# Token rows by transposes, gate products in four column strips: the attention stage of a retention and mixture-of-experts kernel on Trainium2

## The chip, the cores and the metric

One Trainium2 chip, one core. The metric is the device time of one execution in microseconds (us), as a median of runs.

## What is computed

Three layers behind each other, all inputs and outputs in float32:

```python
scores = scale * (q @ k.T)                     # 8 batches, 8 heads, 576 tokens, 64 per head
ret    = scores * Dmat                         # Dmat[i, j] = gamma_h ** (i - j) for i >= j, else 0
x      = (ret @ v), heads side by side         # 4608 token rows of 512
logits = x @ w_gate                            # 8 experts
e      = argmax(logits); g = softmax(logits)[e]
x      = g * (relu(x @ w1[e]) @ w2[e])         # one expert per token
h      = x @ w_in; out = (h * cos(h)) @ w_out
```

## The kernel before

Four stages follow each other on TensorE: attention, the experts, the conversion of the last layer's weights beside them, and the last layer. The change lies in the attention stage, the first 175 us or so.

Attention runs over 40 steps (`steps`), one for each batch and each chunk of 128 tokens (the fifth chunk of a batch has 64). The order of the work is written out by hand: every engine works off its instructions in the order in which the loop at L724 issues them. In step i the loop calls

- `scores(i)` (L452): the products of keys and queries, sixteen float32 matmuls on 64x64 quarters of the array into two PSUM banks, which VectorE multiplies by the mask into `pT` (L466);
- `decay(i + 1)` (L443): the values of the next chunk times a factor per token and head, eight ScalarE multiplications (L449) into `vs`;
- `inter(i - 1)` (L477) and `intra(i - 1)` (L490): the state of earlier chunks times the queries (64x64 quarters, L487), then values times `pT` (two column halves of 64, L497); VectorE multiplies the sum by `gx` into `xt`, features by tokens (L500); L506 adds to the state, which ScalarE copies out (L509);
- `rows(i - 2)` (L511): `xt` is turned into token rows and multiplied by the gate's weights at once. Each of four float32 matmuls has `xt` as the weights and `wgi`, an identity of 128 columns with the 8 gate columns beside it, as the moving operand (L518). ScalarE copies the rows out (L520), VectorE adds up the logits (L521), and SyncE's queue sends the rows to `xd` in HBM (L523).

A float32 matmul stands in the trace as two pairs of weight load and matmul, so the four of L518 are eight records. Every five steps come `route`, `place`, `spread` and `table`, which rank the tokens by expert on VectorE, GpSimd and a few matmuls (L555 to L563, L637). All of `scores`, `rows` and the two blocks turned by `x_block` (L248) near the end take their PSUM banks in turn from one ring of four, tag "sc". Loads of q, k, v have five buffers; the load of step i + 4 is issued at the end of step i (L769), on SyncE's queue behind the rows of step i - 2. Before the loop, L700 to L720 issue the first loads, some memsets and 13 matmuls on zeros (`warm`).

Of the kernel before, what the change touches and what calls it, by code (L numbers as in the profile page):

```python
# [11 lines left out]
F32 = mybir.dt.float32  # L12
# [5 lines left out]
ALU = mybir.AluOpType  # L18
# [4 lines left out]
P = 128  # L23
H = 8
D = 64
DM = 512
E = 8
# [13 lines left out]
NWARM = 13  # L41

# [15 lines left out]
C_TRI = C_GF + NCH * 4  # L58
# [3 lines left out]
C_EYE = C_BASE + E  # L62
C_LO = C_EYE + E
# [40 lines left out]
def of_chunks(q, k, v):  # L104

    B, H_, S, D_ = q.shape

    def turned(x, o, n):
        t = x[:, :, o:o + n].reshape(B, H_ // 2, 2, n, D_).transpose(0, 2, 4, 1, 3)
        return t.reshape(B, 2 * D_, H_ // 2 * n)  # L110

    def rows(x, o, n):
        return x[:, :, o:o + n].transpose(0, 2, 1, 3).reshape(B, n, H_ * D_)

    full = np.stack([np.concatenate([turned(k, o, n), turned(q, o, n), rows(v, o, n), rows(k, o, n)], axis=2)
                     for o, n in CH[:-1]], axis=1)
    o, n = CH[-1]
    return full, np.concatenate([turned(k, o, n), turned(q, o, n)], axis=2), rows(v, o, n)


@with_exitstack
def attn_moe_kernel(ctx, tc, full, part, tail, wg, w1, w2, win, wout, ctab, out):
# [235 lines left out]
    with ExitStack() as actx:  # L358
# [7 lines left out]
        def cc(col, n, rows=P):  # L366
            return ca[:rows, col - C_MASK:col - C_MASK + n]
# [7 lines left out]
        wgs = ap1.tile([P, 4, E], F32, name="wgs")  # L375

        RW = P + E
        wgi = ap1.tile([P, 4, RW], F32, name="wgi")
# [10 lines left out]

        def setup_rows():  # L390
            nc.vector.tensor_copy(out=wgi[:, 0::2, 0:P], in_=ident.unsqueeze(1).to_broadcast([P, 2, P]))
            for a in range(2):
                nc.vector.tensor_copy(out=wgi[:, 1::2, a * D:(a + 1) * D],
                                      in_=ident[:, (1 - a) * D:(2 - a) * D].unsqueeze(1).to_broadcast([P, 2, D]))
            nc.vector.tensor_copy(out=wgi[:, :, P:RW], in_=wgs)
# [15 lines left out]
        for i in range(2):  # L411
            t = ap1.tile([P, NCH, 2, E], F32, name=f"lgt{i}")
            nc.gpsimd.memset(t, 0.0)
            lgt.append(t)
# [96 lines left out]
        def rows(i):  # L511
            b, c = steps[i]
            o, n = CH[c]
            x = ap3.tile([P, 4, P], F32, tag="xs", name="xs")
            for g in range(2):
                two = ps1.tile([P, 4, P], F32, tag="sc", name="rw", bufs=4).rearrange("p (j a) t -> p j (a t)", a=2)
                for j in range(2):
                    mm(out=two[:, j, 0:RW], lhsT=xts[i % 3][:, 2 * g + j, :], rhs=wgi[:, 2 * g + j, :], start=(j == 0),  # L518
                       stop=True, skip_group_check=True)
                nc.scalar.copy(out=x[:n, 2 * g:2 * g + 2], in_=two[:n, :, 0:P])  # L520
                nc.vector.tensor_reduce(out=lgt[b % 2][:n, c, g, :], in_=two[:n, :, P:RW].rearrange("p j e -> p e j"),  # L521
                                        axis=AX.X, op=ALU.add)
            nc.sync.dma_start(out=xd[b * SEQ + o:b * SEQ + o + n, :], in_=x[:n].rearrange("p j t -> p (j t)"))  # L523

# [3 lines left out]
        def route(i0, n):  # L528
# [3 lines left out]
            L = ap2.tile(sh, F32, tag="L", name="L")  # L532
            nc.vector.tensor_add(out=L, in0=lgt[b % 2][:, c0:c0 + n, 0, :], in1=lgt[b % 2][:, c0:c0 + n, 1, :])
# [177 lines left out]
        wgc = wg.rearrange("(c p) e -> p c e", p=P)  # L711
        nc.gpsimd.dma_start(out=wgs[:, 0::2], in_=wgc[:, 0::2])
        for a in range(2):
            nc.gpsimd.dma_start(out=wgs[a * D:(a + 1) * D, 1::2], in_=wgc[(1 - a) * D:(2 - a) * D, 1::2])
# [4 lines left out]
        warm(NWARM, ps1.tile([P, 8, P], F32, tag="x", name="xps").rearrange("p a t -> p (a t)"), idle)  # L719
        decay(0)  # L720
# [3 lines left out]
        for i in range(NS):  # L724
# [23 lines left out]
            if i >= 2:  # L748
                rows(i - 2)
# [684 lines left out]
```

## Time and profile before

| | |
|---|---|
| median of 3 runs | 1383.82 us (1382.86 to 1387.58) |
| the profiled execution | 1377.58 us, span 1375.3 us |
| TensorE matmuls busy | 1354.1 us, 98% of the span |
| TensorE weight loads busy | 1262.5 us, 92% |
| VectorE, ScalarE, GpSimd busy | 68%, 55%, 14% |
| granted TensorE clock, mean | 0.996 |
| moved by DMA | 300.58 MB, mean 219 GB/s |

The profile shows one execution, and its rows carry times from the span's start. PE is TensorE's matmuls, PEld its weight loads, DVE VectorE, ACT ScalarE, POOL GpSimd and SP SyncE. A matmul's duration in a row is its latency: matmuls overlap, so what one costs is read from start to start. A row for a stretch has its start and end, its length, the busy time of PE, PEld, DVE, ACT and POOL, each with its count of instructions, the granted TensorE clock, the busy share of the DMA engines and GB/s. A number in square brackets is idle time before, with what ended it.

### The profile page before, as it was taken

To read this page: it belongs to the slowest core of one execution; us is meant where nothing else is said; L and a number is where in the kernel's file an instruction comes from. 1 tells how busy PE (TensorE), PEld (TensorE's weight loads), DVE (VectorE), ACT (ScalarE), POOL (GpSimd) and SP (SyncE) were. 2 spreads that over 40 slices of the span, in tenths; PEclk is the share of its full clock that TensorE was granted. 3 is DMA by queue.
4 is the path that set the end of the run, shared out by engine and by line. 5 is a ranking of instruction groups with operands and counts; after the bars stand their busy time and mean duration, and the time that the engine had idled before them with its cause. 6 is when DMAs were issued, how large, how long until landed. Compare 5 with 4: busy or idle time off the path is not lost.

```text
span 1375.3 us, 28314 instructions
## 1 busy us (share of the span) xinstructions
PE 1354.1 (98%) x11234; PEld 1262.5 (92%) x11234; DVE 939.5 (68%) x1928; ACT 757.2 (55%) x1687; POOL 191.0 (14%) x300
## 2 busy tenths in 40 slices
PE   7999999999999999999999999999999999999998
PEld 6888899999999999998999999999999999999997
DVE  4777865867778687847666676766767676666655
ACT  5788725444544455336556555555555555555544
POOL 4334530121211212100010100101001010010101
PEclk9999999999999999999999999999999999999999
DMA  8899626575876668976564655646455564564551
GB/s 290 320 329 346 213 61 217 180 262 183 285 246 203 211 230 268 331 275 259 176 258 164 220 190 191 220 166 249 183 192 201 194 233 161 209 226 162 196 184 57
DMA packets 72648, 300.58 MB, mean 219 GB/s; under 512 B 7748, under 2 KB 15904, under 8 KB 58560
## 3 DMA queue, kind: packets, MB, share of 16 engines
q1 hardware_dynamic: 60000, 256.18, 53.0%
q0 software_dynamic: 12512, 42.56, 8.3%
q8 instruction: 89, 1.46, 0.4%
q14 instruction: 47, 0.39, 0.1%
HBM read 247.24 MB, written 51.47 MB: 217 GB/s over the span
## 4 chain that ended last, share of the span: by engine, by line
PE 49%; issue 6%; POOL 0%; POOLq 0%; ACT 0%
PE acc L1341 25%; PE hps L1265 24%; POOL out_dram L1323 0%; POOLq L1430 0%; ACT ka L1295 0%; POOL spare L159 0%; PE acc L1352 0%; POOLq L1323 0%; ACT orow L1321 0%
## 5 line engine op out<-in xcount | busy, mean ns | idle before, releaser
L1341 PE MATMUL acc<-wunit,gh 128*128 128x512 f32 x1152 | 358.2, 392 | 0.0
L1265 PEld LDWEIGHTS hps<-far,wquad 128*128 128x128 f32 x2064 | 261.8, 191 | 8.0 <-ACTq L1239 0.7
L1265 PE MATMUL hps<-far,wquad 128*128 128x256 f32 x2064 | 266.7, 283 | 0.5 <-ACTq L1239 0.5
L1341 PEld LDWEIGHTS acc<-wunit,gh 128*128 128x128 f32 x1152 | 207.2, 189 | 36.0
L1341 PE MATMUL acc<-wunit,gl 128*128 128x512 f32 x576 | 224.3, 389 | 0.0
L274 PE MATMUL hps<-xT,wunit 128*128 128x256 f32 (+6 forms) x1536 | 209.4, 297 | 0.5 <-ACT yev L291 0.5
L274 PEld LDWEIGHTS hps<-xT,wunit 128*128 128x128 f32 x1536 | 206.7, 188 | 0.9 <-ACT yev L291 0.7
L289 PE MATMUL hps<-hh,wunit 128*128 128x256 f32 (+6 forms) x960 | 197.9, 301 | 0.0
L289 PEld LDWEIGHTS hps<-hh,wunit 128*128 128x128 f32 x960 | 155.8, 190 | 0.1
L289 PE MATMUL hps<-hl,wunit 128*128 128x256 f32 (+6 forms) x480 | 143.5, 299 | 1.4 <-DVE hl L278 1.4
L1323 POOL DMA_INDIRECT out_dram<-orow,perm x36 | 35.4, 982 | 740.3 <-DVE orow L1319 736.4
L1341 PEld LDWEIGHTS acc<-wunit,gl 128*128 128x128 f32 x576 | 108.2, 188 | 24.5 <-DVE gl L1308 0.8
L1306 ACT CAST gh<-sa 128x512 fp32r<-128x512 f32 x144 | 89.6, 622 | 72.9 <-DVE sa L1302 72.9
L1302 DVE SCALAR_TENSOR_TENSOR sa<-sa,box 128x512 f32<-128x512 f32 x144 | 99.0, 688 | 42.8 <-ACT sa L1300 41.7
L1265 PE MATMUL hps<-near,wquad 128*128 128x256 f32 x960 | 126.6, 283 | 0.0
L1265 PEld LDWEIGHTS hps<-near,wquad 128*128 128x128 f32 x960 | 123.1, 191 | 3.6
L1276 DVE TENSOR_TENSOR box<-hps,box 128x256 f32<-128x256 f32 x72 | 30.6, 424 | 136.7 <-PE hps L1265 136.5
L1308 DVE TENSOR_TENSOR gl<-sa,gh 128x512 fp32r<-128x512 f32 x144 | 98.9, 687 | 18.5 <-ACT gh L1306 12.9
L1297 DVE SCALAR_TENSOR_TENSOR sa<-box,ka 128x512 f32<-128x512 f32 x144 | 98.9, 687 | 12.4 <-ACT ka L1295 12.3
L1275 ACT COPY box<-hps 128x256 f32<-128x256 f32 x72 | 26.8, 372 | 141.3 <-PE hps L1265 132.5
L1021 DVE TENSOR_TENSOR wunit<-wst,wunit 128x512 fp32r<-128x512 f32 x112 | 75.2, 686 | 36.9 <-ACT wunit L1020 36.8
L1299 ACT ACTIVATE sa<-sa 128x512 f32<-128x512 f32 x144 | 91.2, 634 | 8.6 <-DVE sa L1297 8.6
(217 smaller groups left out, 1877.4 us busy)
## 6 DMA issues: line engine op xcount, KB each, us to landing
wquad<-ws SPq DMA_DIRECT2D x72, 1792.0 KB
wst<-in_moe_w_dram SPq DMA_DIRECT2D x64, 512.0 KB
ld<-in_full_dram SPq DMA_DIRECT2D x29, 1024.0 KB
ws<-cvo POOLq DMA_DIRECT2D x28, 512.0 KB, 3.5
xd<-xs SPq DMA_DIRECT2D x32, 256.0 KB
cvw<-in_moe_w_in_dram SPq DMA_DIRECT2D x16, 512.0 KB
cvw<-in_moe_w_out_dram SPq DMA_DIRECT2D x16, 512.0 KB
wd<-cvo POOLq DMA_DIRECT2D x16, 512.0 KB, 5.3
```

Of the source, the lines that this page charges most:

```text
L274: mm(out=ph[:, :n], lhsT=u[:, a, kc, f0:f0 + P], rhs=t[:, bq, kc, :n], start=(idx == 0), stop=(idx == 11))
L289: mm(out=py[:, :n], lhsT=u[:, w], rhs=t[:, :n], start=(fc == 0 and g == 0), stop=(fc == 7 and g == 2))
L1021: nc.vector.tensor_sub(out=u[:, 1, 2 * g + c], in0=s[:, c], in1=u[:, 0, 2 * g + c])
L1265: mm(out=o, lhsT=u[:, s, kc, a], rhs=x[:, bq, kc], start=(s in (0, 1, 2) and idx == 0), stop=(idx == 5), skip_group_check=True)
L1276: nc.vector.tensor_add(out=u2, in0=y[:, :HT], in1=p1)
L1297: nc.vector.scalar_tensor_tensor(out=sa, in0=x, scalar=INV2PI, in1=ka, op0=ALU.mult, op1=ALU.subtract)
L1299: nc.scalar.activation(out=sa, in_=sa, func=AF.Sin, scale=math.pi)
L1302: nc.vector.scalar_tensor_tensor(out=sa, in0=sa, scalar=-1.0, in1=x, op0=ALU.add, op1=ALU.mult)
L1306: nc.scalar.copy(out=gh, in_=sa)
L1308: nc.vector.tensor_sub(out=gl, in0=sa, in1=gh)
L1323: ins = nc.gpsimd.indirect_dma_start(out=out[:, :], out_offset=bass.IndirectOffsetOnAxis(ap=perm[:, k:k + 1], axis=0), in_=o, in_offset=None)
L1341: mm(out=acc2[T][c], lhsT=pair[n][:, fh, c % 2 * P:(c % 2 + 1) * P], rhs=u[:, w, fc % 4], start=(q == 0 and fh == 0 and n == 0 and w == 0) ...
```

## The change

- `rows` turns `xt` into token rows by four transposes in transpose mode (L533 of the new file), and the gate's product is taken apart from it: four matmuls, one for each 128 features, each into its own strip of 32 PSUM partitions (L526). ScalarE copies the strips out (`quarters`), and a new function `logits` adds them by one matmul against stacked identities (L541), of which VectorE copies 8 columns out.
- `rows(i - 2)` moves from the end of the step to right behind `scores(i)`; `logits(i - 2)` stands behind `intra(i - 1)`.
- The rows now hold the features in the order of `xt`, and the gate's weights and `w1` are laid out on the host in that order (`of_gate`, `of_first`). The table `wgi` and its set-up go, and so does the addition of two halves of the logits in `route`.
- `decay`: in the first three steps (`OWN`) VectorE scales a chunk's values in one instruction; from then on ScalarE scales four heads and GpSimd the other four.
- Loads before the loop stand in another order, the gate's weights come by SyncE's queue, a first ScalarE instruction on one element stands ahead of all (L718), and six more matmuls on zeros behind `scores(0)`.

```diff
+def of_gate(w):
+
+    t = w.reshape(4, 2, D, E).copy()
+    t[1::2] = t[1::2, ::-1]
+    out = np.zeros((P, 4, 32), w.dtype)
+    out[:, :, :E] = t.reshape(4, P, E).transpose(1, 0, 2)
+    return out.reshape(P, 4 * 32)
...
-        wgs = ap1.tile([P, 4, E], F32, name="wgs")
+        wgs = ap1.tile([P, 4, 32], F32, name="wgs")
         def decay(i):
             vs = ap3.tile([P, H, D], F32, tag="vs", name="vs", bufs=4) if n == P else halfv[b % 2]
-            for h in range(H):
+            h0 = 0 if i < OWN else H // 2
+            for h in range(h0):
                 nc.scalar.mul(vs[:n, h], s["v"][:n, h], cc(C_GK + c * H + h, 1, n))
+            (nc.vector if i < OWN else nc.gpsimd).tensor_tensor(
+                out=vs[:n, h0:], in0=s["v"][:n, h0:],
+                in1=cc(C_GK + c * H + h0, H - h0, n).unsqueeze(2).to_broadcast([n, H - h0, D]), op=ALU.mult)
         def rows(i):
-            x = ap3.tile([P, 4, P], F32, tag="xs", name="xs")
-            for g in range(2):
-                two = ps1.tile([P, 4, P], F32, tag="sc", name="rw", bufs=4).rearrange("p (j a) t -> p j (a t)", a=2)
-                for j in range(2):
-                    mm(out=two[:, j, 0:RW], lhsT=xts[i % 3][:, 2 * g + j, :], rhs=wgi[:, 2 * g + j, :], start=(j == 0),
-                       stop=True, skip_group_check=True)
-                nc.scalar.copy(out=x[:n, 2 * g:2 * g + 2], in_=two[:n, :, 0:P])
-                nc.vector.tensor_reduce(out=lgt[b % 2][:n, c, g, :], in_=two[:n, :, P:RW].rearrange("p j e -> p e j"),
-                                        axis=AX.X, op=ALU.add)
+            xt = xts[i % 3]
+            lt = ps1.tile([P, 4, P], F32, tag="sc", name="lt", bufs=4)
+            for j in range(4):
+                mm(out=lt[32 * j:32 * j + 32, 0, :], lhsT=wgs[:, j, :], rhs=xt[:, j, :], start=True, stop=True,
+                   skip_group_check=True)
+            quarters = ap2.tile([P, P], F32, tag="lts", name="lts")
+            nc.scalar.copy(out=quarters, in_=lt[:, 0, :])
+            st[i]["lt"] = lt, quarters
+            two = ps1.tile([P, 4, P], F32, tag="sc", name="rw", bufs=4)
+            for j in range(4):
+                nc.tensor.transpose(two[:, j, :], xt[:, j, :], ident)
+            x = ap3.tile([P, 4, P], F32, tag="xs", name="xs")
+            nc.scalar.copy(out=x[:n], in_=two[:n])
             nc.sync.dma_start(out=xd[b * SEQ + o:b * SEQ + o + n, :], in_=x[:n].rearrange("p j t -> p (j t)"))
+        def logits(i):
+            lt, quarters = st[i].pop("lt")
+            mm(out=lt[:, 1, 0:E], lhsT=quarters, rhs=cc(C_EYE, E), start=True, stop=True, skip_group_check=True)
+            nc.vector.tensor_copy(out=lgt[b % 2][:, c, :], in_=lt[:, 1, 0:E])
...
+        nc.scalar.mul(spare, one[0:1], one[0:1])
         load(0, (0, 2))
         nc.sync.dma_start(out=ca[:, :C_TRI - C_MASK], in_=ctab[:, C_MASK:C_TRI])
+        load(1, (0, 2))
         load(0, (2, 3))
-        load(1, (0, 2))
+        load(0, (3, 4))
         nc.sync.dma_start(out=gx[:, 0].rearrange("p j t -> p (j t)"), in_=ctab[:, C_GX:])
-        load(0, (3, 4))
         load(1, (2, 4))
         load(2, (0, 2))
         nc.sync.dma_start(out=ct, in_=ctab[:, :C_MASK])
+        nc.sync.dma_start(out=wgs.rearrange("p c e -> p (c e)"), in_=wg)
         load(2, (2, 4))
         load(3)
...
             scores(i)
-            if i + 1 < NS:
+            if i < OWN:
+                decay(i)
+            if i == 0:
+                warm(NWARM // 2, blank, idle)
+            if OWN <= i + 1 < NS:
                 decay(i + 1)
-            if i == 1:
-                setup_rows()
+            if i >= 2:
+                rows(i - 2)
             if i >= 1:
                 inter(i - 1)
                 intra(i - 1)
+            if i >= 2:
+                logits(i - 2)
...
-            if i >= 2:
-                rows(i - 2)
...
+        rows(NS - 2)
         inter(NS - 1)
         intra(NS - 1)
-        rows(NS - 2)
+        logits(NS - 2)
         table(*waiting.pop())
         layer1(0, 0, 0)
         rows(NS - 1)
+        logits(NS - 1)
         route(*groups[NS - 1])
```

On TensorE, a full step and the scores behind it, in the middle of attention. The file before (sc are the scores, xps the sum, S the state, rw the rows):

```order
L462 MATMUL sc<-ld 64x128 x16
L487 MATMUL xps<-ld,sbd_136 64x128 x8
L497 MATMUL xps<-pT,vs 64x128 x8
L506 MATMUL S<-vs,ld 64x64 x8
L518 MATMUL rw<-wgi,xt_130 128x136 x4
L462 MATMUL sc<-ld 64x64 x8
```

The changed file (lt are the gate's strips, then the logits):

```order
L471 MATMUL sc<-ld 64x128 x16
L526 MATMUL lt<-xt_129,wgs 32x128 x4
L533 MATMUL rw<-ct,xt_129 128x128 x4
L496 MATMUL xps<-ld,sbd_135 64x128 x8
L506 MATMUL xps<-pT,vs 64x128 x8
L515 MATMUL S<-vs,ld 64x64 x8
L541 MATMUL lt<-ca,lts 128x8
L471 MATMUL sc<-ld 64x64 x8
```

The rows moved from between S and the scores to between the scores and xps, and one matmul stands now where they stood.

On ScalarE, from the start of the program to the rows of the second step that has them. Before:

```order
L449 ACT_TABLE_LOAD
L449 ACTIVATE vs<-ld,ca 128x64 x24
L509 COPY sbd_136<-S 128x256
L449 ACTIVATE vs<-ld,ca 128x64 x8
L509 COPY sbd_137<-S 128x256
L520 COPY xs<-rw 128x256 x2
L449 ACTIVATE halfv_142<-ld,ca 64x64 x8
L509 COPY sbd_136<-S 128x256
L520 COPY xs<-rw 128x256 x2
```

Changed:

```order
L718 ACT_TABLE_LOAD
L718 ACTIVATE spare<-biases 1x1
L518 COPY sbd_135<-S 128x256
L455 ACTIVATE vs<-ld,ca 128x64 x4
L529 COPY lts<-lt 128x128
L535 COPY xs<-rw 128x512
L518 COPY sbd_136<-S 128x256
L455 ACTIVATE halfv_139<-ld,ca 64x64 x4
L529 COPY lts<-lt 128x128
L535 COPY xs<-rw 128x512
```

The three scalings ahead of the first copy of the state are gone from this queue, and the strips' copy (lts) stands behind the scaling of the next chunk.

On TensorE, the last full step of attention, where `x_block` turns a block (xturn) out of the same ring of banks, in the changed file:

```order
L541 MATMUL lt<-ca,lts 128x8
L273 MATMUL xturn<-ct,xrow 128x128 x4
L471 MATMUL sc<-ld 64x64 x8
L526 MATMUL lt<-xt_131,wgs 32x128 x4
L533 MATMUL rw<-ct,xt_131 128x128 x4
```

Before, xps (24 matmuls with the state's) stood between these scores and the rows; now only the strips do.

## Rows read from the trace of the kernel before

**Rows 1.** One batch of five steps: start:end, length, busy time by engine.

```profile
102.04:121.53 19.49, 19.49 (x408) 17.68 (x405) 15.81 (x48) 16.30 (x59) 8.22 (x14) 1.00 0.96 340
```

**Rows 2.** PE in order of time, two steps: start, us, instructions.

```profile
113.64 1.10 PE L462 MATMUL sc<-ld 64*64 64x128 f32 x32
114.68 1.09 PE L497 MATMUL xps<-pT,vs 128*64 128x128 f32 x16
...
116.17 1.19 PE L518 MATMUL rw<-wgi,xt 128*128 128x136 f32 x8
117.29 1.10 PE L462 MATMUL sc<-ld 64*64 64x128 f32 x32
118.21 0.62 PE L487 MATMUL xps<-ld,sbd 64*64 64x128 f32 x16
118.76 1.09 PE L497 MATMUL xps<-pT,vs 128*64 128x128 f32 x16
119.69 0.64 PE L506 MATMUL S<-vs,ld 128*64 128x64 f32 x16
120.25 1.19 PE L518 MATMUL rw<-wgi,xt 128*128 128x136 f32 x8
121.28 0.18 PE L555 MATMUL lg<-rbase,ones 128*128 128x40 bf16 x1
...
121.36 0.24 PE L563 MATMUL lg<-ohb,ones 128*128 128x32 bf16 x4
121.53 1.10 PE L462 MATMUL sc<-ld 64*64 64x128 f32 x32
```

**Rows 3.** PE in order of time, rows followed by a block's transposes.

```profile
165.03 0.51 PE L518 MATMUL rw<-wgi,xt 128*128 128x136 f32 x3
165.38 0.60 PE L256 MATMUL xturn<-ct,xrow 128*128 128x128 f32 x4
165.91 0.62 PE L462 MATMUL sc<-ld 64*64 64x64 f32 x13
```

**Rows 4.** PE in order of time, three short matmuls of the ranking.

```profile
186.66 0.51 PE L637 MATMUL lg<-rt,oh 128*128 128x40 f32 x3
187.09 0.38 PE L289 MATMUL hps<-hidden,wunit 128*128 128x256 f32 x1
```

**Rows 5.** Groups of ACT and POOL, 82.25 to 121.53: busy, mean ns, idle before.

```profile
L449 ACT ACTIVATE vs<-ld,ca 128x64 f32<-128x64 f32 x64 | 16.2, 337 | 2.6 <-DMA ld<-in_full_dram 2.5
L520 ACT COPY xs<-rw 128x256 f32<-128x256 f32 (+1 forms) x22 | 8.1, 370 | 2.2 <-PE rw L518 0.7 <-ACT vs L449 0.3
...
L583 POOL TENSOR_TENSOR hot<-hot,ge 128x200 f32<-128x200 f32 x2 | 1.2, 609 | 0.2
```

**Rows 6.** ACT and PE in order of time, 12.7 to 21.3, the start.

```profile
18.98 2.02 ACT L449 ACTIVATE vs<-ld,ca 128x64 f32<-128x64 f32 x8 [1.01 <-DMA ld<-in_full_dram]
...
18.02 0.67 PE L487 MATMUL xps<-ld,sbd 64*64 64x128 f32 x16 [2.68 <-ACT sbd L509]
...
21.23 0.34 PE L462 MATMUL sc<-ld 64*64 64x128 f32 x4
```

**Rows 7.** The slowest batch as a stretch, and its longest stall on PE and ACT.

```profile
51.59:74.36 22.77, 20.30 (x405) 17.98 (x405) 15.90 (x49) 17.08 (x65) 8.03 (x14) 1.00 0.89 305
...
60.85 0.39 PE L506 MATMUL S<-vs,ld 128*64 128x64 f32 x6 [1.67 <-issue]
...
60.46 2.02 ACT L449 ACTIVATE vs<-ld,ca 128x64 f32<-128x64 f32 x8 [3.57 <-DMA ld<-in_full_dram]
```

**Rows 8.** The turned block's last reader on DVE, and PE's group of the rows.

```profile
169.01 0.68 DVE L260 TENSOR_TENSOR xT<-xturn,xT 128x512 fp32r<-128x512 f32 x1
...
L518 PE MATMUL rw<-wgi,xt 128*128 128x136 f32 x320 | 47.9, 292 | 0.6 <-DVE xT L260 0.6
```

**Rows 9.** Two stretches: the second step's scores at the start, and one with transposes.

```profile
9.90:11.90 2.00, 2.00 (x34) 1.67 (x36) 0.00 (x0) 1.93 (x8) 1.18 (x2) 0.50 1.04 371
165.00:168.00 3.00, 3.00 (x61) 2.66 (x61) 2.10 (x11) 1.46 (x4) 1.42 (x4) 1.00 0.25 87
```

More of the change, by code (lines that the diff above doesn't have):

```diff
@@ L41 @@
 NWARM = 13
+OWN = 3
 INV2PI = 1.0 / (2.0 * math.pi)
@@ L57 @@
 C_GF = C_GK + NCH * H
-C_TRI = C_GF + NCH * 4
+C_EYE = C_GF + NCH * 4
+C_TRI = C_EYE + E
 C_ONE = C_TRI + 128
@@ L61 @@
 C_BASE = C_REV + NCH * E
-C_EYE = C_BASE + E
-C_LO = C_EYE + E
+C_LO = C_BASE + E
 C_IOTA = C_LO + E * NBLK
@@ L118, in of_chunks, with of_first @@
     return full, np.concatenate([turned(k, o, n), turned(q, o, n)], axis=2), rows(v, o, n)
+def of_gate(w):
[4 more added lines that the diff above has]
+    return out.reshape(P, 4 * 32)
+def of_first(w):
+    t = w.reshape(E, 4, 2, D, F1).copy()
+    t[:, 1::2] = t[:, 1::2, ::-1]
+    return t.reshape(E, DM, F1)
 @with_exitstack
@@ L388, in setup_ranking @@
             nc.vector.memset(rsb, 0.0)
[L390 to L395, printed above, removed]
         def decay_table(c):
@@ L411, in attn_moe_kernel @@
         for i in range(2):
-            t = ap1.tile([P, NCH, 2, E], F32, name=f"lgt{i}")
-            nc.gpsimd.memset(t, 0.0)
-            lgt.append(t)
+            lgt.append(ap1.tile([P, NCH, E], F32, name=f"lgt{i}"))
         halfv = [ap1.tile([P, H, D], F32, name=f"halfv{i}") for i in range(2)]
@@ L513, in rows @@
             o, n = CH[c]
-            x = ap3.tile([P, 4, P], F32, tag="xs", name="xs")
-            for g in range(2):
-                two = ps1.tile([P, 4, P], F32, tag="sc", name="rw", bufs=4).rearrange("p (j a) t -> p j (a t)", a=2)
-                for j in range(2):
-                    mm(out=two[:, j, 0:RW], lhsT=xts[i % 3][:, 2 * g + j, :], rhs=wgi[:, 2 * g + j, :], start=(j == 0),
-                       stop=True, skip_group_check=True)
-                nc.scalar.copy(out=x[:n, 2 * g:2 * g + 2], in_=two[:n, :, 0:P])
-                nc.vector.tensor_reduce(out=lgt[b % 2][:n, c, g, :], in_=two[:n, :, P:RW].rearrange("p j e -> p e j"),
-                                        axis=AX.X, op=ALU.add)
-            nc.sync.dma_start(out=xd[b * SEQ + o:b * SEQ + o + n, :], in_=x[:n].rearrange("p j t -> p (j t)"))
+            xt = xts[i % 3]
[9 more added lines that the diff above has]
+                nc.tensor.transpose(two[:, j, :], xt[:, j, :], ident)
+            x = ap3.tile([P, 4, P], F32, tag="xs", name="xs")
+            nc.scalar.copy(out=x[:n], in_=two[:n])
+            nc.sync.dma_start(out=xd[b * SEQ + o:b * SEQ + o + n, :], in_=x[:n].rearrange("p j t -> p (j t)"))
+        def logits(i):
+            b, c = steps[i]
+            lt, quarters = st[i].pop("lt")
+            mm(out=lt[:, 1, 0:E], lhsT=quarters, rhs=cc(C_EYE, E), start=True, stop=True, skip_group_check=True)
+            nc.vector.tensor_copy(out=lgt[b % 2][:, c, :], in_=lt[:, 1, 0:E])
         def cst(col, c0, n):
@@ L531, in route @@
             sh = [P, n, E]
-            L = ap2.tile(sh, F32, tag="L", name="L")
-            nc.vector.tensor_add(out=L, in0=lgt[b % 2][:, c0:c0 + n, 0, :], in1=lgt[b % 2][:, c0:c0 + n, 1, :])
+            L = lgt[b % 2][:, c0:c0 + n, :]
             mx = ap2.tile([P, n], F32, tag="mx", name="mx")
@@ L708, in attn_moe_kernel @@
         nc.sync.dma_start(out=ct, in_=ctab[:, :C_MASK])
+        nc.sync.dma_start(out=wgs.rearrange("p c e -> p (c e)"), in_=wg)
         load(2, (2, 4))
         load(3)
[L711 to L714, printed above, removed]
         for c in range(1, NCH):
@@ L718, in attn_moe_kernel @@
         nc.vector.memset(idle, 0.0)
-        warm(NWARM, ps1.tile([P, 8, P], F32, tag="x", name="xps").rearrange("p a t -> p (a t)"), idle)
-        decay(0)
+        blank = ps1.tile([P, 8, P], F32, tag="x", name="xps").rearrange("p a t -> p (a t)")
+        warm(NWARM, blank, idle)
         wq = dict(zip((6, 7, 11, 15, 16, 21, 25, 26), [(key, g) for key in w_units(0) for g in range(2)]))
@@ L1418 @@
     laid = dict(zip(("full", "part", "tail"), of_chunks(inputs['q'], inputs['k'], inputs['v'])))
+    laid["moe_w_gate"] = of_gate(inputs["moe_w_gate"])
+    laid["moe_w1"] = of_first(inputs["moe_w1"])
     for name in ["full", "part", "tail"] + _INS:
```

2 lines of the change are left out of this document (removed).

## The prediction

> **What bounds the kernel now.** I read the page's busy shares first (the table above has them), then the busy times of one batch, then TensorE in order of time. In the batch from 102.04 to 121.53 us TensorE's matmuls are busy for all of its 19.49 us [rows 1]; VectorE has 15.81 of it, ScalarE 16.30, GpSimd 8.22, and the DMA engines are busy 96%. So a steady step costs what its matmuls cost from start to start, and whatever else the change does counts only where TensorE waits.
>
> In a full step [rows 2] the scores take 0.92 us (117.29 to 118.21), the products with the state 0.55, values 0.93, the state's update 0.56, and the rows 1.03 or 1.12. The two figures for the rows are the first thing to see. Where the next matmul also works on the whole 128x128 array (the ranking, at 121.28), the rows cost 1.03; where scores on 64x64 quarters follow (116.17 to 117.29), 1.12. In the same way scores cost 0.92 ahead of matmuls on 64x64 quarters and 1.04 ahead of values on 128x64 halves (113.64 to 114.68). **Leaving one division of the array for another costs 0.09 to 0.12 us**, and it costs more behind it: eight records of the rows follow each other at 0.116 us (three from 165.03 to 165.38, [rows 3]), which makes 0.93, and the group has 1.03. The other 0.10 is the first weight load of 128 columns, which nothing covers; for 64 columns I take 0.05.
>
> **The change, part by part.** *Removed from each step*: the rows, 1.12 us.
>
> *Added: the gate's product.* Four float32 matmuls are eight records of 128 columns, 32 weights wide, in four strips. Wherever the trace divides the array, the parts work side by side: 32 records of scores in four quarters take 0.92, 16 of values in two halves 0.92 to 0.93 [rows 2], thus about 0.11 for a wave of either kind. So I take two waves, 0.22, with 0.05 for the first weights and 0.09 for leaving: 0.36. The ends: 0.31 if the short weight load is hidden; 0.58 if only two strips run together, as halves do; 1.02 if the eight come one by one.
>
> On four strips, the Trainium skill says less: "TensorE: Matmul & The Clock Gate", Part 3, Measured speedup vs the span model, has 2.38 times for three column strips. By that figure a wave would be an estimated quarter longer, the gate 0.06 dearer, and the predicted time 2 us higher. The quarters and halves of this trace show no such loss, so the sum goes without it.
>
> *Added: the transposes.* Four in transpose mode are one record each, not two: 0.60 for four with a latency of 0.27 each, so 0.11 apart [rows 3]. With 0.10 for the first weights and 0.09 for leaving: 0.63. They alone would save half of the rows' time.
>
> *Added: the logits' matmul.* Two records with weights of 128 columns and 8 columns to multiply. Nearest are three of 40 columns, in 0.43 [rows 4]; I take 0.10, 0.11 and 0.03 for two weight loads and the short tail, and 0.09 for leaving: 0.33. The lower end is bfloat16's 0.04 each (four from 121.36 to 121.53, [rows 2]): 0.17.
>
> *Moved: the rows behind the scores.* Scores and products with the state, both on quarters, stood next to each other for nothing. Now the scores are left for strips (0.12) and the products with the state entered from transposes (0.05). Before there were three divisions a step, now there are six.
>
> Sum of a full step: 0.12 + 0.36 + 0.63 + 0.05 + 0.33 - 1.12 = +0.37; I take 0.36, since the 0.12 and 0.05 are rounded up. In the step at the start of a batch the scores were followed by another division anyway: 0.36 + 0.63 + 0.33 - 1.12 = +0.20.
>
> *Between the fourth step's scores (21.23, [rows 6]) and the last's (165.91, [rows 3])* lie 36 steps, 7 of them first of a batch: 29 x 0.36 + 7 x 0.20 = **+11.8 us**.
>
> *ScalarE and GpSimd.* ScalarE loses four of eight scalings, which are 2.02 us for eight [rows 6], so 1.0 a step, and gains a copy of 128x128 (under the 0.37 of 128x256, [rows 5]); GpSimd gains one 128x256 product, an estimated 0.8 from 0.61 for 128x200 [rows 5], some 4 us on its 8.2 of a batch. None of the three bounds a step. The scaled values of step i + 1 are used two steps later, 8 us, longer than the ranking (about 8 us in five steps) holds GpSimd. So nothing is won and nothing lost here. VectorE loses one short instruction in a step: nothing.
>
> *The start.* Before, TensorE waits 2.68 us at 18.02 for the copy of the state, which stands on ScalarE behind three scalings [rows 6]. Those three are now VectorE's, so this wait goes. But the next one is near: the strips' copy stands behind the scaling of step 3's values, and their load lands at 18.98 [rows 6]. From there 1.0 for four scalings, 0.3 for the copy, 0.3 for the logits and 0.1 for leaving make 20.8 for the fourth step's scores, against 21.23: **-0.4 us**. Loads in another order and six warm matmuls lie ahead of that and change nothing.
>
> *Stalls on loads.* Five steps around the longest one (1.67 at 60.85, as ScalarE waits 3.57 for a load) take 22.77 us, 3.3 over the steady 19.49 [rows 7]. All 36 steps take 144.7, and 7.2 steady batches would be 140.3, so 4.4 is all that stalls cost. Longer steps give each load more time, and its issue no longer stands behind rows that end the step. I take **-3 us**; the ends are 0 and -4.4.
>
> *The end.* The last step's transposes take the bank that the block turned before them holds. Its last reader on VectorE, L260, ends at 169.69 [rows 8], behind routing instructions that start when the logits are there. Before, the rows met it late and waited 0.6; now they stand ahead of values and state, some 2 us earlier, and wait an estimated 1.9: +1.3. The last full step adds 0.36, two more sets of rows beside 128x128 matmuls 0.2 each: **+2 us**.
>
> Sum: 11.8 - 0.4 - 3 + 2 = +10.4, I say +10. Behind attention TensorE is busy throughout, so this reaches the end: 1387.6 on the profiled execution's 1377.58, and on the median of 1383.82, 6 us above it, **1393.5 us**.
>
> **Rivals.**
>
> *Faster: new divisions are free.* If a strip's weights and the transposes' slipped in behind the last matmul without a pause, only the work would differ: 0.22 + 0.44 + 0.14 - 0.93, -0.13 in a step, -5 in all; with -0.4, -3 and a neutral end about -8, 1376. It decides as soon as a new division costs under some 0.05 in all. Against it: every change of division in [rows 2] pays, halves to whole array too. Chance 0.13.
>
> *No difference: the logits at bfloat16's price.* 0.17 instead of 0.33 makes the full step +0.20 and the first of a batch +0.04: 6 us; with all stalls gone (-4.4), -0.4 and 1.5 at the end, +3, 1386.5. For it: the columns are few. Against: [rows 4]. Chance 0.16.
>
> *Slower still: strips do not run four at a time.* Two together: +0.22 in each of 40 steps, 1402; one by one, +0.65, 1420. The trace has no strips of 32, and four strips of 128 partitions read twice what two halves do. Chance 0.11.
>
> *The strips' copy behind a late load.* ScalarE must have the values of step i + 1 before it copies the strips of step i - 2, and TensorE waits for these at the end of the same step, not in the next. If loads come no earlier against their step than now, the 2.5 us that ScalarE waits in two batches [rows 5] reach TensorE: up to 10 us, 1403. Chance 0.06.
>
> *The clock falls.* Transposes stand in the trace at full clock: the four at 165.38 [rows 3] lie in a stretch that was granted 1.00, which is 2.4 GHz [rows 9]. In the changed kernel they are a seventh of each step, with more pauses. At a granted 0.50, 1.2 GHz, the second step's scores take 2.00 us for what takes 1.10 later ([rows 9], [rows 2]); 160 us of attention so would be some 120 us more, 1510. Chance 0.02. The same page of the Trainium skill, Part 4: PE-mode transpose, says that transposes don't count as activity for the clock; four transposes in 3 us neither show nor contradict that.
>
> **How the numbers follow.** A measurement of this kernel tells 0.3%, 4 us, from no change. My forecast has 0.52 and by itself 1388 to 1400 (logits or stalls at either end); the rivals have 0.13, 0.16, 0.11, 0.06 and 0.02. Slower: 0.52 + 0.11 + 0.06 + 0.02 = 0.71; same 0.16; faster 0.13. The range of 8 in 10 takes in the case of no difference, most of the strips in pairs and of the late load: 1382 to 1406; it leaves out 0.13 below and some 0.06 above.
>
> **What would show it.** Right: in a steady step TensorE is busy without a pause; six groups, the gate near 0.36 from start to start, the transposes 0.63, the logits 0.33; a steady batch of 21.1 us instead of 19.49; no wait for the copy of the state at the start; the last step's transposes waiting for L277, as L260 is called there. The forecast is wrong if a batch stays at 19.5 or less, if the transposes start within 0.1 us of the last strip, or if TensorE's wait in a step is for a copy or a load rather than for the array.

## The result and the profile after

| | before | after |
|---|---|---|
| median, runs on the same chip | 1382.86 us (1380.55 to 1387.58) | 1396.07 us (1389.78 to 1396.77) |
| ratio of the runs, with its 95% interval | | 1.0088 [1.0059, 1.0118] |
| span of the profiled execution | 1375.3 us | 1394.3 us |

The changed kernel is slower by 0.9%; the forecast was 1393.5 us, in a range of 1382 to 1406. The profiled executions lie 19 us apart, the medians 13: the one before was quicker than any of its five runs, the one after is their median.

One batch of five steps after the change, as a stretch (start:end, length, busy time by engine, granted clock, busy share of the DMA engines, GB/s):

```profile
129.10:149.99 20.89, 20.89 (x438) 17.07 (x435) 15.77 (x42) 11.88 (x39) 11.15 (x19) 1.00 0.88 307
```

As in [rows 1], TensorE is busy for all of the batch, and the batch is 1.4 us longer. ScalarE has 4.4 us less to do in it and GpSimd 2.9 more; none of the other engines comes near TensorE's share. TensorE in order of time, one full step and the scores behind it:

```profile
129.10 1.10 PE L471 MATMUL sc<-ld 64*64 64x128 f32 x32
130.13 0.43 PE L526 MATMUL lt<-xt,wgs 128*32 128x128 f32 x8
130.49 0.66 PE L533 MATMUL rw<-ct,xt 128*128 128x128 f32 x4
131.07 0.67 PE L496 MATMUL xps<-ld,sbd 64*64 64x128 f32 x16
131.67 1.09 PE L506 MATMUL xps<-pT,vs 128*64 128x128 f32 x16
132.59 0.63 PE L515 MATMUL S<-vs,ld 128*64 128x64 f32 x16
133.16 0.39 PE L541 MATMUL lt<-ca,lts 128*128 128x8 f32 x2
133.48 0.68 PE L471 MATMUL sc<-ld 64*64 64x64 f32 x16
```

From start to start: scores 1.03, strips 0.36, transposes 0.58, products with the state 0.60, values 0.92, state 0.57, logits 0.32; 4.38 in all. In [rows 2] such a step is 4.08 with the rows at 1.12. The eight records of the strips run four at a time: in the trace four of them start within 0.02 us, and the other four 0.13 later.

The start, ScalarE and TensorE in order of time, and TensorE's clock behind it as a stretch:

```profile
18.35 1.06 ACT L455 ACTIVATE vs<-ld,ca 128x64 f32<-128x64 f32 x4 [6.36 <-DMA ld<-in_full_dram]
19.32 0.24 ACT L529 COPY lts<-lt 128x128 f32<-128x128 f32 x1
...
19.62 0.39 PE L541 MATMUL lt<-ca,lts 128*128 128x8 f32 x2 [2.40 <-ACT lts L529]
19.93 1.78 PE L471 MATMUL sc<-ld 64*64 64x128 f32 x32
```

```profile
20.00:24.00 4.00, 4.00 (x61) 2.80 (x60) 1.46 (x3) 2.13 (x8) 2.46 (x5) 0.57 0.93 317
```

The wait for the state's copy [rows 6] is gone. In its place TensorE waits 2.40 us for the strips' copy, which stands behind a scaling that waits for a load, and then runs near its lower level (1.2 GHz). The fourth step's scores come 1.3 us sooner than before, the fifth's 0.5 later (25.82 against 25.31).

The longest stall of the steady part, TensorE in order of time, and the DMA queues' packets, MB and share from 94.40 to 96.86:

```profile
94.40 0.33 PE L506 MATMUL xps<-halfpT,halfv 128*64 128x64 f32 x2
96.86 0.68 PE L506 MATMUL xps<-halfpT,halfv 128*64 128x64 f32 x14 [2.13 <-issue]
```

```profile
q1 hardware_dynamic: 203, 0.88, 95.4%
q8 instruction: 1, 0.02, 2.4%
```

TensorE stops within one group of matmuls, where no load or copy is missing ("issue"), and in that time the one packet of the instruction queue lands (94.50 to 95.43), amid transfers of data that take nearly all the rest of the DMA engines' time. The stall in [rows 7] is of the same kind: such a packet ends 1.5 us before TensorE goes on.

The end of attention, VectorE and TensorE:

```profile
177.95 0.68 DVE L277 TENSOR_TENSOR xT<-xturn,xT 128x512 fp32r<-128x512 f32 x1
...
178.68 0.66 PE L533 MATMUL rw<-ct,xt 128*128 128x128 f32 x4 [2.04 <-DVE xT L277]
```

The last full step's transposes wait for the block's last reader, as foreseen. The first matmul of the experts (L291) behind attention starts at 212.95, against 201.14 (L274 before). From there the profiled executions part by another 7 us: 5.6 in the experts, in which the change alters no instruction, and 1.5 in the last layer.

### The profile page after: what moved, and what is told of

Same layout as the page of the kernel before. It is cut to its first block, busy times and chain, and to the rows that moved or that the text cites. A ratio compares the mean times of both kernels' runs of the same rounds, so it can differ in the third digit from the quotient of the medians.

```text
span 1394.3 us, 28707 instructions
## 1 busy us (share of the span) xinstructions
PE 1366.9 (98%) x11480; PEld 1258.4 (90%) x11480; DVE 939.0 (67%) x1878; ACT 720.3 (52%) x1516; POOL 212.4 (15%) x332
## 4 chain that ended last, share of the span: by engine, by line
PE 48%; issue 6%; DMA 1%; POOL 0%; POOLq 0%; ACT 0%
PE acc L1363 25%; PE hps L1287 23%; DMA wquad<-ws 1%; POOL out_dram L1345 0%; POOLq L1454 0%; ACT ka L1317 0%; POOL spare L176 0%; POOLq L1345 0%; ACT orow L1343 0%
## 5 line engine op out<-in xcount | busy, mean ns | idle before, releaser
L291 PE MATMUL hps<-xT,wunit 128*128 128x256 f32 (+6 forms) x1536 | 210.0, 297 | 1.9 <-DVE hl L295 1.4
L291 PEld LDWEIGHTS hps<-xT,wunit 128*128 128x128 f32 x1536 | 206.8, 189 | 2.8 <-DVE hl L295 2.0
```

The source lines that it names most:

```text
L291: mm(out=ph[:, :n], lhsT=u[:, a, kc, f0:f0 + P], rhs=t[:, bq, kc, :n], start=(idx == 0), stop=(idx == 11))
```

## The experiments

The theory was the price of each new division of the array. Rivals were the rest of the change (loads and scaling), waits for copies and loads, and, once the stalls were seen, TensorE's own instructions. Each group ran on one chip together with the kernel before: the first four of the table; the three without loads and late scaling; the others, with a second execution of both kernels.

| kernel | median, us | ratio to before, 95% interval |
|---|---|---|
| strips between | 1387.36 | 1.0044 [1.0023, 1.0065] |
| strips between, turned | 1385.79 | 1.0045 [1.002, 1.0071] |
| strips of two steps | 1388.41 | 1.0061 [1.0041, 1.0082] |
| old rows | 1378.42 | 0.998 [0.9963, 0.9997] |
| late scaling | 1385.1 | 1.0033 [1.0015, 1.0052] |
| late scaling, turned | 1381.15 | 0.9997 [0.9978, 1.0015] |
| old rows, late scaling | 1385.34 | 1.0034 [1.0022, 1.0045] |

### Strips between: the same matmuls, fewer divisions

The strips stand between the products with the state (quarters) and the values (halves), the transposes behind the state's update, next to the logits.

```diff
-            if i >= 2:
-                rows(i - 2)
             if i >= 1:
                 inter(i - 1)
+            if i >= 2:
+                strips(i - 2)
+            if i >= 1:
                 intra(i - 1)
             if i >= 2:
+                rows(i - 2)
                 logits(i - 2)
```

> The changed kernel with its gate strips moved between the products with the state and the values, and its rows and logits back at the end of the step; the same instructions. Theory (each change of the array's division costs 0.15 to 0.2 us, with the first weights): four divisions a step instead of six, a full step of 4.14 us instead of 4.37, the last step's wait of 2.0 for the ring's bank under 0.7; 36 steps save about 7, the end 1.4: some 9 us under the changed kernel, near 1387. Rival (the strips, transposes and copies cost as work, wherever they stand): a full step of 4.3 to 4.4, 1394 to 1397.

TensorE in order of time, one full step:

```profile
101.29 1.10 PE L471 MATMUL sc<-ld 64*64 64x128 f32 x32
102.21 0.62 PE L496 MATMUL xps<-ld,sbd 64*64 64x128 f32 x16
102.76 0.43 PE L524 MATMUL lt<-xt,wgs 128*32 128x128 f32 x8
103.11 1.09 PE L506 MATMUL xps<-pT,vs 128*64 128x128 f32 x16
104.04 0.63 PE L515 MATMUL S<-vs,ld 128*64 128x64 f32 x16
104.60 0.65 PE L536 MATMUL rw<-ct,xt 128*128 128x128 f32 x4
105.09 0.29 PE L544 MATMUL lt<-ca,lts 128*128 128x8 f32 x2
```

With every record still there, scores cost 0.92 instead of 1.03, products with the state 0.55 instead of 0.60, transposes 0.49 instead of 0.58, logits 0.22 instead of 0.32 where scores follow (101.07 to 101.29, the step before): 0.35 less, the price of the divisions that this order saves. That makes a full step of 4.03, shorter than before. Over 36 steps this should have won some 12 us; by the ratios, half of that came (1.0088 to 1.0044). So the median is where it was expected, but by luck: the step won 0.35 us and not the 0.23 that was expected, and waits took half of it back. TensorE's waits show where. This execution is the slowest of the kernel's seven, 6.7 us over their median, so it may show more of them than most:

```profile
20.69 0.60 PE L544 MATMUL lt<-ca,lts 128*128 128x8 f32 x2 [3.97 <-ACT lts L527]
46.69 0.49 PE L536 MATMUL rw<-ct,xt 128*128 128x128 f32 x3 [1.37 <-issue]
53.37 0.34 PE L496 MATMUL xps<-ld,sbd 64*64 64x64 f32 x5 [1.22 <-issue]
61.25 0.77 PE L471 MATMUL sc<-ld 64*64 64x128 f32 x20 [1.06 <-issue]
67.83 0.66 PE L496 MATMUL xps<-ld,sbd 64*64 64x128 f32 x13 [1.30 <-issue]
```

Counted from the start of the program, weight loads, matmuls and the instructions between them that wait for semaphores, the four "issue" stalls stand at TensorE's instructions 1473, 1729, 1985 and 2242: 256 apart, to within one.

### Strips between, turned by a transpose

```diff
-            mm(out=lt[:, 1, 0:E], lhsT=quarters, rhs=cc(C_EYE, E), start=True, stop=True, skip_group_check=True)
-            nc.vector.tensor_copy(out=lgt[b % 2][:, c, :], in_=lt[:, 1, 0:E])
+            nc.tensor.transpose(lt[:, 1, :], quarters, ident)
+            nc.vector.tensor_reduce(out=lgt[b % 2][:, c, :], in_=lt[:, 1, :].rearrange("p (j e) -> p e j", j=4)[:, 0:E, :],
+                                    axis=AX.X, op=ALU.add)
```

and `logits` stands ahead of `rows`.

> As gate_between, and the strips' sum by one transpose of the copied strips and a reduction on VectorE instead of a float32 matmul against identities. Theory: one weight load of 0.11 instead of two, behind other whole-array work, so 0.1 less a step: 4.04, as before the change, and with the earlier start some 2 us under the kernel before or level with it, 1380 to 1385. Rival (work, not divisions): still 5 us or more over before, 1388 to 1394.

Between the two. The steps are a little shorter (4.01), but the wait for the strips' copy at the start is 4.30, in four batches TensorE waits 0.59 to 0.98 for it, and four stalls 256 instructions apart or a multiple of it add 3.6.

### Strips of two steps together

`strips` for two steps in one bank, in every second step, then both turnings and both sets of rows.

```diff
+            of = () if i < 2 else (i - 2,) if i > 35 else (i - 3, i - 2) if i % 2 else ()
+            if of:
+                strips(*of)
```

> As gate_between_turned, with the strips, logits and rows of two steps at once in every second step, up to the 36th. Theory: the strips' and the transposes' divisions are paid once in two steps, about 0.95 us a step for rows and logits where the kernel before has 1.12: a batch of 18.6 to 18.9 instead of 19.49, 1374 to 1379, faster than both. Rival (work, or the ring of four banks, which three banks at once overfill): waits for banks in each second step, 1384 or more.

Missed, and the time is the rival's. The two turnings share a bank, and in nearly every pair the second waits, mostly 0.28, for VectorE's reading of the first; stalls of TensorE's instructions take 3.4 more. What two steps together cost without that was not tried.

### Old rows: the rest of the change alone

The kernel before with the loads' order, the scaling on VectorE and GpSimd and the extra matmuls on zeros.

```diff
-            for h in range(H):
+            h0 = 0 if i < OWN else H // 2
+            for h in range(h0):
                 nc.scalar.mul(vs[:n, h], s["v"][:n, h], cc(C_GK + c * H + h, 1, n))
+            (nc.vector if i < OWN else nc.gpsimd).tensor_tensor(
...
+        nc.scalar.mul(spare, one[0:1], one[0:1])
...
+            if i == 0:
+                warm(NWARM // 2, blank, idle)
```

> The kernel before with only the rest of the change: order of the loads, first three scalings on VectorE, half of the others on GpSimd, one ScalarE instruction ahead, six more warm matmuls; rows and gate as before, three divisions. Theory: nothing of the loss is here; the fourth step's scores 1 to 1.5 us earlier than 21.2, a batch of 19.5, 1379 to 1384. Rival (GpSimd's or VectorE's share of the work, or the loads' order, costs): a batch of 20 or more, 1388 or more.

The theory held in that the rest costs nothing: by the ratio this version is some 3 us ahead of the kernel before, the quickest of all. So the whole loss comes with the new rows and the gate. Where the gain comes from isn't shown. The earlier start that was expected is not in the profile: the fourth step's scores stand at 21.50 and not 1 to 1.5 us ahead of 21.2, as TensorE was granted 0.50 from 14.6 to 21.5; and a batch takes 19.8 us for 19.5, with a wait of 0.27 for the ranking's table.

### Without the loads of q, k and v, three kernels

From step 5 on each step works on the data of steps 0 to 4.

```diff
             s = st[i]
+            if i > 4:
+                s.update((k, st[i - 5][k]) for k in ("ld", "kT", "qT", "v", "k"))
+                return
             if "ld" not in s:
```

> The kernel before without the loads of q, k and v from the sixth step on: steps 5 to 39 work on the data of steps 0 to 4, so this computes other numbers. Every "issue" stall of TensorE in the attention stages so far stands at an instruction count that is a multiple of 256 behind the first one (1473, 1729, 1985, ...), right behind a 16 KB transfer of the instruction queue. Theory: these stalls are TensorE's own instructions coming late, because the loads fill the DMA engines. Then no such stall is left here, and with the 3 us that they and the colder clock cost in the kernel before gone, the time is 3 to 4 us under the kernel before, 1376 to 1379. Rival: the stalls belong to the program (a block's end always costs something), and the time stays within 1.5 us of the kernel before.

> The changed kernel without the loads of q, k and v from the sixth step on, with other numbers computed, as in the first. Theory: the price of the change is what TensorE's instructions cost from start to start: 0.30 in a full step, 0.13 in the first of a batch, so 9.6 over 36 steps, 0.5 at the start, 2.1 at the end; 12 us over the same edit of the kernel before, with no stall at a block of instructions, a steady batch of 20.7 to 20.9, and scores of the last step 10 us behind. Rival: the change's price lies in stalls on loads; then without loads it is under 8 us.

> The version with the gate's strips between the products with the state and values, and the transposes beside the logits, without the loads of q, k and v from the sixth step on, with other numbers computed. Theory: its steps are shorter than those before (4.03 against 4.08, a batch of 19.3 against 19.5 to 19.8), and what kept it from showing this is late instructions (over 10 us of stalls and cold clock in its profile). Without loads these go: 9 to 11 us under its own 1387, and within 2 us of the same edit of the kernel before. Rival: the stalls come with the shorter steps themselves, whatever the loads do, and it stays 5 us or more over the edited kernel before.

The medians are 1702.13, 1712.34 and 1697.2 us. They aren't comparable with the others: with other data the stages behind attention differ, and TensorE waits 195 to 197 us at one place there. Only attention is read, and the times against each other. From the fifth step's scores to the last's as one stretch, of the three in that order:

```profile
25.91:162.48 136.57, 136.29 (x2830) 123.61 (x2829) 107.68 (x329) 113.38 (x405) 54.64 (x92) 1.00 0.31 98
```

```profile
24.66:169.47 144.81, 144.81 (x3039) 118.67 (x3039) 105.56 (x289) 81.65 (x264) 73.65 (x125) 1.00 0.28 93
```

```profile
25.27:159.63 134.36, 134.36 (x3039) 117.60 (x3038) 105.49 (x288) 83.16 (x264) 73.58 (x124) 1.00 0.31 100
```

The DMA engines are busy 28 to 31% instead of 90, and no stall at a block of instructions is left in any of the three. (One "issue" gap of 0.28 remains, at 152.05 in the kernel before. It isn't at such a count, and with loads it is there too, 0.27 at 155.40: another kind, against what was expected of every "issue" stall.) What remains is the bare price of the steps: 35 of them cost 8.2 us more after the change, and 2.2 less with the strips between. The experts begin at 197.68, 208.22 and 194.51. The first two medians differ by 10.2 us, where 12 was said and the rival had under 8; the third lies 4.9 under the first, further than the 2 that was said. Up to the experts' first matmul, the kernel before loses 3 us to its loads and the version with strips between 17, the waits at the start included, in its slowest execution. The absolute times expected of the three can't be read here.

All fourteen profiles, counted in the trace from 25 to 175 us: stalls of 0.25 us or more within one instruction of a multiple of 256 from the 1473rd.

| kernel | stalls | us |
|---|---|---|
| before, two executions | 1, 1 | 1.7, 0.6 |
| after, two executions | 2, 1 | 2.4, 0.5 |
| old rows; the same, late scaling | 1; 0 | 1.0; 0 |
| strips between; turned; two steps | 8; 4; 4 | 9.0; 3.6; 3.4 |
| late scaling; turned | 6; 6 | 5.7; 5.5 |
| without loads, three kernels | 0, 0, 0 | 0 |

Where the row of such a stall names an engine (three of them name VectorE, one ScalarE), its place in the count is the same. And in all 34 TensorE goes on 1.2 to 1.55 us behind the end of a packet of the instruction queue; for its other waits of this length the distance to the last packet is anything from 0.0 to 7.2. So it is the packet that it waited for. The page of the changed kernel, TensorE's busy times with their instructions and the instruction queue with its packets and MB:

```profile
PE 1366.9 (98%) x11480; PEld 1258.4 (90%) x11480; DVE 939.0 (67%) x1878; ACT 720.3 (52%) x1516; POOL 212.4 (15%) x332
...
q8 instruction: 91, 1.49, 0.4%
```

22,960 weight loads and matmuls, with 197 instructions that wait or branch, make 254 to each of 91 packets of 16 KB. So TensorE's instructions come in blocks of 256, and a block may come late while loads fill the DMA engines. The counts agree with a simple reading: in a batch without stalls TensorE works off some 42 weight loads and matmuls a microsecond before and after the change, and 45 with the strips between, and the kernels at 42 have 0 to 2 stalls, the five with the strips between 4 to 8. But each count is of one execution, and no run changed the rate alone, so that a higher rate causes the stalls is not shown. Nor do these runs show which queue inside the DMA engines holds the block back.

### Late scaling

The strips between, with the scaling behind the copies.

```diff
-            if OWN <= i + 1 < NS:
-                decay(i + 1)
...
                 rows(i - 2)
                 logits(i - 2)
+            if OWN <= i + 1 < NS:
+                decay(i + 1)
```

> The version with the gate's strips between the products with the state and values, with the scaling of the next step's values behind the copies of strips and rows on ScalarE and GpSimd, instead of ahead of them. Theory: the 4 us that TensorE waited at 20.7 for the strips' copy, and the half clock behind it, came from the strips' copy standing behind a scaling that waits for a load. Now the fourth step's scores stand at 18.4 to 19 (their own load lands at 18.3), the fifth's at 24 instead of 27.3, and the time is 3 us under that version, 1384. Rival: the load decides anyway, or the scaling now holds the copy of the state of the next step: then no gain, 1386 to 1389.

TensorE at the start:

```profile
17.18 0.29 PE L544 MATMUL lt<-ca,lts 128*128 128x8 f32 x2
19.31 1.13 PE L471 MATMUL sc<-ld 64*64 64x128 f32 x31 [1.85 <-DMA ld<-in_full_dram]
```

The strips' copy no longer waits: the fourth step's scores stand at 19.31 and wait for their own load, the fifth's at 23.42 instead of 27.34, at full clock. The median moved by 2.3 us of the 3 expected (1387.36 to 1385.1), but on another chip; the ratio moved by less, and the two intervals overlap. So the wait is gone, and a gain in time is not clear of the noise.

### Late scaling, turned

The same edit as in the turned version above, with `rows` still ahead of `logits`.

> The version with the strips between the products with the state and values and the late scaling, where the strips are now turned back by one transpose (in transpose mode, one record instead of two) that VectorE adds up four by four, instead of a matmul against stacked identities. Theory of the steps alone: 0.1 less in each step, a steady batch of 18.8 to 19.0 instead of 19.3, so 4 us under the late scaling's 1385, 1381. Rival, by the stalls: a shorter step reaches the end of its block of instructions sooner, the loads keep the DMA engines as full as before, and half or more of it is waited away again: 1383 to 1386.

By the median the theory of the steps is met (1381.15, and by the ratios 5 us less than without the turning); two batches without a stall are 19.1 and 19.2, just over the 18.8 to 19.0 that was said. The stalls stayed (six of 5.5 us, six of 5.7 without the turning) but took no more, so the rival didn't show here. With strips, transposes and all, this version is level with the kernel before. Three of its stalls, TensorE in order of time:

```profile
49.52 0.42 PE L524 MATMUL lt<-xt,wgs 128*32 128x128 f32 x5 [0.96 <-issue]
74.71 0.72 PE L506 MATMUL xps<-pT,vs 128*64 128x128 f32 x9 [1.81 <-issue]
87.76 0.38 PE L496 MATMUL xps<-ld,sbd 64*64 64x128 f32 x2 [0.43 <-issue]
```

### Old rows, late scaling

```diff
-            if OWN <= i + 1 < NS:
-                decay(i + 1)
...
+            if OWN <= i + 1 < NS:
+                decay(i + 1)
             if i + 4 < NS:
                 load(i + 4)
```

> The kernel before with the rest of the change (order of loads, half of the scaling on GpSimd), and the scaling moved to the end of the step. Theory: its rows take the fewest of TensorE's instructions, so its blocks of 256 last longest and come late least; and with GpSimd's scaling behind the ranking of the same step, the 0.27 us that TensorE waited in each batch for the ranking's table goes: 2 us under the version without the move, 1376 to 1378, ratio 0.996 to 0.998 and the fastest of all. Rival: the scaling is now late for the step that uses it, or nothing was won since the ranking's wait only moves: 1378 to 1381.

Missed, on the rival's side and beyond it. GpSimd and TensorE in order of time:

```profile
109.48 0.72 POOL L631 TENSOR_TENSOR rt<-hot,gh 128x200 fp32r<-128x200 f32 x1
...
110.16 0.52 POOL L631 TENSOR_TENSOR rt<-hot,gl 128x200 fp32r<-128x200 f32 x1
...
110.64 0.60 POOL L452 TENSOR_TENSOR halfv<-ld,ca 64x256 f32<-64x256 f32 x1
...
111.30 0.45 PE L502 MATMUL xps<-halfpT,halfv 128*64 128x64 f32 x8 [1.08 <-POOL halfv L452]
```

GpSimd's scaling now stands behind the whole ranking of the step, and TensorE waits 1.05 to 1.11 us for it in each batch. Six such waits are 6.5 us, and the version lost 7 by the medians. The 0.27 that the ranking's table had cost was the cheaper of the two.

### A second look at both kernels

Both kernels as they are, one execution each.

> The kernel before, unchanged, for a second look. In the profiles so far the stage of the experts takes 409.4 us before the change, 415.0 after it, and 411.7 to 415.4 in the other versions, with no instruction of that stage changed. Theory: this is the spread from one execution to the next (waits for loads and copies that fall one way or the other), and a second execution of the kernel before lies at 411 to 413. Rival: it is a cost of the change, and it stays at 409 to 410.

> The changed kernel, unchanged, for a second look. Theory: stalls at blocks of TensorE's instructions differ from one execution to the next, in place and in length, while the steps' own lengths stay as they are: the steady batch is 20.7 to 20.9 again, the "issue" stalls stand at other multiples of 256 and add up to something between 1 and 6 us; the experts take 412 to 415. Rival: the stalls at 88 and 97 us come back at the same place.

TensorE at the first matmul of the experts and at the first of the last layer, of the kernel before:

```profile
200.57 2.73 PE L274 MATMUL hps<-xT,wunit 128*128 128x360 f32 x15 [0.51 <-ACT yev L291]
...
613.92 0.38 PE L1265 MATMUL hps<-far,wquad 128*128 128x256 f32 x1 [0.49 <-ACTq L1239]
```

and of the changed one:

```profile
212.14 2.07 PE L291 MATMUL hps<-xT,wunit 128*128 128x360 f32 x11 [0.51 <-ACT yev L308]
...
625.28 1.46 PE L1287 MATMUL hps<-far,wquad 128*128 128x256 f32 x10 [0.49 <-ACTq L1261]
```

The experts take 413.4 us before the change and 413.1 after it, where the first profiles had 409.4 and 415.0. So that difference was spread between executions (the 413.4 is a little over the 411 to 413 expected), and the change's part is what stands at the experts' first matmul, 11.6 us here and 11.8 in the first pair, with some part of the last layer. That takes 764.8 us in both executions before and 766.3 in both after. 0.7 of it lies behind the last matmul, where GpSimd pauses 1.3 us ahead of its last transfer instead of 0.2; there the seven profiles with the new gate and all loads have 6.8 to 6.9 us, the four with the old rows 6.1. Another 0.7 to 0.8 is a wait for the layer's weights (0.79 at 642.36 in the first), which both versions of the old rows have too, shorter or longer. No run shows why. The stall of the changed kernel comes elsewhere (52.02) and is 0.5 in all, less than the 1 to 6 expected; its batches without a stall are 20.7 again, and its time is 1.0088 of the median before on this chip too.

## Why the prediction was right

Sign, size and the main mechanism, the price of the divisions, came out. Two terms were off in opposite directions, 11.8 for 8.5 and -3 for 0, and that they nearly cancel is luck.

*Removed and added.* The strips' 0.36 was exact, the logits 0.32 for 0.33, leaving the scores 0.11 for 0.12, entering the products 0.05 as said. The transposes measured 0.58 for 0.63: +0.30 in a full step, not +0.36. The fifth step of a batch, whose logits stand ahead of the ranking on the whole array, pays only 0.24 for them; I had given it a full step's price. The first step of a batch pays 0.13 for 0.20. So a batch costs 1.24 more (20.72 against 19.48 without loads) and not 1.6, and the term of **+11.8 us for 36 steps should have been 8.5**: 8.2 measured over 35, and 0.3.

On column strips the Trainium skill ("TensorE: Matmul & The Clock Gate", Part 3, Measured speedup vs the span model) has 2.38 times for three, measured with 512 columns, which had made the gate an estimated 0.42. The 0.36 of the trace doesn't bear that out for four strips of 128 columns, and the measurement decides.

*The start, -0.4.* The wait for the strips' copy behind the late load came where it was put. The fourth step's scores came at 19.93, sooner than the 20.8 said, but the clock fell behind the wait, which the sum hadn't counted. At the fifth step's scores the kernels are level: +0.5 in the first pair of profiles, -0.5 in the second.

*Stalls on loads, -3.* **This step failed.** I took the stall of 1.67 at 60.85 for a wait for q, k and v, which more time would have covered, because ScalarE waited for a load beside it. It was a wait for TensorE's own instructions. From the fifth scores to the last the kernel before takes 140.6 and 139.3, against 136.6 without loads: 4.0 and 2.7 lost. After the change it is 149.8 and 146.4 against 144.8: 5.0 and 1.5. Set beside the same kernel without loads, the stretches of late instructions make up 1.9 of the 4.0, 0.9 of the 2.7, 3.0 of the 5.0 (with 1.5 more at half clock behind the stall) and 0.5 of the 1.5; the rest is short waits, the largest for VectorE at 55 to 57 us before the change (0.8 to 0.9). None of TensorE's waits in these stretches names a load directly. So nothing was relieved that the noise between executions would let one see, and 0, the upper end that I gave, was right.

*The end, +2.* The wait of 2.04 (1.9 said) is there in both executions. From the last step's scores to the experts' first matmul it makes +2.1 in one, and +5.0 in the other, where the clock fell behind it.

The terms as measured are 8.5, 0, 0 and 2 to 5, so 10.5 to 13.5 in place of +10. The sum had nothing behind attention, and there the last layer took 1.5 more in both pairs of profiles. With it they part by 13.3 and 13.0, the experts left out; the medians differ by 13.2.

*Slips in the sums.* 18.98 and the four pieces behind it make 20.7, not 20.8, and +10 on the median of 1383.82 makes 1393.8, not 1393.5. Neither changes the argument.

*The rivals.* Free divisions fell: the same records in another order cost 0.35 less in a step. The logits at bfloat16's price and strips in pairs fell in the first profile. The strips' copy behind a late load is true at the start and, in the changed kernel, not later. In attention the clock fell only behind waits of TensorE, and a batch with four transposes in each step was granted 1.00.

## What to carry to other kernels

On a saturated TensorE, count a step's changes between divisions of the array as well as its matmuls: here each cost 0.05 to 0.12 us, and the order of the same seven groups was worth 0.35 of 4.4. Before shortening steps in a stage whose loads keep the DMA engines 90% busy, look for "issue" stalls inside a group of matmuls and count TensorE's instructions between them, those that wait for semaphores too: where they stand at equal counts, each behind a packet of the instruction queue, the instructions themselves come late. Here a shorter step with as many instructions gave half of its gain back, part of it to such stalls. A profile is one execution; the experts, which the change doesn't touch, moved by 4 us between two executions of one kernel, so a second look comes before a story about it.

## What was not expected of the hardware

TensorE's instructions come in blocks of 256 (16 KB). With the DMA engines some 90% busy a block came up to 2.1 us late; at 30% none did, in one execution each of three kernels. The clock's answer to a wait was not the same each time: the wait of 2.0 us at the end of attention left the clock as it was in one execution of the changed kernel and halved it in the other, as the stretches show (the first profile, then the second):

```profile
176.00:180.00 4.00, 1.96 (x40) 1.28 (x38) 3.08 (x12) 1.14 (x3) 3.18 (x7) 1.00 0.01 4
```

```profile
176.00:180.00 4.00, 4.00 (x50) 3.49 (x49) 0.69 (x1) 0.59 (x1) 1.29 (x3) 0.50 0.18 70
```

In the first the wait ends at 178.68, in the second at 175.02.
